# First loads, warm-up products, the second chunk's normalization and the last products of a fused attention and squared-ReLU layer, reordered

## The chip, the core and the metric

The kernel runs on one core of one Trainium2 chip. The metric is the device time of one execution in microseconds (us); lower is better. A profiled execution gives a trace, whose times start at the first instruction. The engines are named as in the profile: PE (TensorE matmul), PEld (its weight load), DVE (VectorE), ACT (ScalarE), POOL (GpSimd), SP (SyncE, which issues most DMAs).

## What is computed

```python
xn = layernorm(x)                                   # x: 2048 x 512
q, k, v = split(xn @ wqkv)                          # 32 heads of 16
s = softmax(q k^T / 4) v, heads joined, @ wo
g = silu(relu(xn @ w1 + b1)**2 @ w2 + b2)           # 512 -> 1792 -> 512
out = x + s * g
```

All of it is float32. The kernel reaches that accuracy by splitting each operand of a linear product into a high part (a cast to the format fp32r) and a low part (the operand less the high part) and adding three products: high by high, high by low, low by high.

## The kernel before

The 2048 rows are worked in four chunks (c = 0 to 3) of 512 rows, each of four tiles of 128 rows. The kernel has three stages. The first, up to about 140 us, normalizes the chunks and makes values, keys and queries. The second, most of the time, runs scores, exponentials and products with the values in 128 turns, with the other branch's matmuls between them. The third, the last 20 us, projects what is left and writes the output. The order of instructions on each engine is the order of the program text (a manual schedule); an engine that waits holds everything behind it in its own queue.

**First loads** (`load_x` L127, `load_w` L140, L427 to L431). SP issues the first chunk's tile 0 and tile 1 as two DMAs of 256 KB (L135), then the upper half of the value weights (L136, `load_w("v", sp, (0,))`), tiles 2 and 3 (one DMA of 512 KB, L132), the lower half of the value weights, the key weights, chunk 1 and b1; the query weights follow at L446.

**Warm-up** (L437 to L439). Eleven products of the identity with itself, into a bank that nobody reads. The profile shows each as two instructions.

**Normalization** (`norm` L162). A generator of three steps: statistics on DVE (L169), their aggregation on DVE and a square root on ACT (L172, L176), and the reciprocal, a correction of three small DVE instructions and the normalized tile on DVE (L178 to L186). `next(parts)` runs one step where it stands.

**Chunk 0** (L440 to L464). `split_w("v", (k,))` (L155) casts slice k of the weights on ACT (L98, tile `wf1h`) and makes the low part on POOL (L104, `wf1l`). `transpose_tile(i)` (L212) transposes tile i of the first pair on PE (L217), copies the high part on ACT (L219, tile `KA`) and makes the low part on DVE (L220). Then two accumulations of twelve products each are interleaved (L458 to L460, the products at L111), twenty of them ahead of the transposes of tiles 2 and 3 (`transpose(0, 1)`, L197 to L210, PE line L204). The order of ACT's queue is: slice 0, tile 0, slice 1, tile 1, square root for tiles 2 and 3, slices 2 and 3.

**The loop over the chunks** (L472 to L512). For each chunk: values tile by tile (`end_value`, L238), then for each g of 0 to 3 the keys and the queries (`keyquery`, L245: twelve products on PE, a cast on ACT, L98, a subtraction on DVE, L104, a DMA on SP). Between them stand steps of the next chunk's normalization (`parts`). For chunk 0, three of the six steps for chunk 1 run behind the values of tiles 2 and 3, and three behind the keys and queries of g = 0 and the keys of g = 1. At g = 2 the next chunk is transposed (L492 to L494).

**The end** (L812 to L864). `end_rest(i, src)` (L740) scales a finished projection of tile i of chunk 2 on DVE (L743) and has POOL issue a DMA that adds it to the output (L744). `h` and `l` are high and low part of the last head's normalized result (L843 to L846); `nvalid` (L847) is the flag that decides whether the general path runs; it does not run here. The last four tiles, those of chunk 3, each take three products (L657 in `group`), a DVE multiplication by the gate (L859), and an addition of x. The products are made in pairs of tiles: both high products of two tiles, then the low product of each. Tile 0's addition is POOL's, those of tiles 2 and 3 are DVE's (L863), and tile 1 is added by a DMA that POOL issues (L861) to what `add_gated` (L645, L651) wrote there in the second stage. ACT issues the other three output DMAs (L864).

Of the kernel before, what the change touches and what calls it, by code (L numbers as in the profile page):

```python
# [28 lines left out]
OP = mybir.AluOpType  # L29
# [8 lines left out]
NC = S // 512  # L38
# [35 lines left out]
def fast_path(tc, sb, ps, env):  # L74
    nc = tc.nc
    ident, vt, nvalid, stat = (env[n] for n in ("ident", "vt", "nvalid", "stat"))
    kdram, qdram, xdram, udram, zdram, gdram = (
        env[n] for n in ("kdram", "qdram", "xdram", "udram", "zdram", "gdram"))
    x, wqkv, wo, w1, b1, w2, b2, out = (
        env[n] for n in ("x", "wqkv", "wo", "w1", "b1", "w2", "b2", "out"))  # L80
    mm = nc.tensor.matmul
    dve, act, pool, sp = nc.vector, nc.scalar, nc.gpsimd, nc.sync
# [3 lines left out]
    def t(shape, dt, tag):  # L86

        cnt[0] += 1
        p = ps if tag in ("S", "lin", "acc") else sb
        if tag in BUFS:  # L90
            turn[tag] = turn.get(tag, -1) + 1
            n = turn[tag] % BUFS[tag]
            tag = f"{tag}{places[n] if tag == 'S' else n}"
        return p.tile(shape, dt, tag=tag, name=f"{tag}_{cnt[0]}")
# [19 lines left out]
    def run(gen):  # L114
        for _ in gen:
            pass
# [10 lines left out]
    def load_x(c):  # L127
        for i in range(2):
            a = xload[c, i] = t([128, 2, 512], FT, f"P{4 + 2 * (c % 2) + i}")
            r = c * 512 + i * 256  # L130
            if c or i:
                sp.dma_start(a, x[r:r + 256].rearrange("(a p) d -> p a d", p=128))  # L132
            else:
                for j in range(2):
                    sp.dma_start(a[:, j], x[128 * j:128 * j + 128])  # L135
                load_w("v", sp, (0,))  # L136

    w_tags = {"v": "wf1", "k": "wf2", "q": "h"}
# [1 line left out]
    def load_w(which, eng, parts=range(2)):  # L140
        o = {"q": 0, "k": 512, "v": 1024}[which]
        if which in wraw:
            pass
        elif which == "v":
            a = t([128, 4, 512], FT, "KA2")
            wraw[which] = [a[:, :2], a[:, 2:]]
        elif which == "k":
            wraw[which] = [t([128, 2, 512], FT, "QA") for _ in range(2)]
        else:
            wraw[which] = [t([128, 2, 512], FT, "wr") for _ in range(2)]  # L150
        for i in parts:
            eng.dma_start(wraw[which][i], wqkv[i * 256:i * 256 + 256, o:o + 512]
                          .rearrange("(a p) f -> p a f", p=128))

    def split_w(which, ks=range(4)):  # L155
        if which not in wsp:
            tiles = [[t([128, 2, 512], FR, f"{w_tags[which]}{p}{i}") for i in range(2)] for p in "hl"]
            wsp[which] = [[a[k // 2][:, k % 2] for k in range(4)] for a in tiles]
        for k in ks:
            split(wsp[which][0][k], wsp[which][1][k], wraw[which][k // 2][:, k % 2], act, pool)  # L160
# [51 lines left out]
    def transpose_tile(i):  # L212

        h, low = xT[0]
        pt = t([128, 4, 128], FT, "S")
        for k in range(4):
            nc.tensor.transpose(pt[:, k], xnorm[0, 0][:, i, 128 * k:128 * k + 128], ident)  # L217
        s = slice(128 * i, 128 * i + 128)
        act.copy(h[:, :, s], pt)  # L219
        dve.tensor_tensor(low[:, :, s], pt, h[:, :, s].bitcast(FT), op=OP.subtract)  # L220
# [214 lines left out]
        pool.memset(part[:, :, H * 17:], 0.0)  # L435
    pool.memset(stat, 1.0)
    idle = t([128, 512], FT, "lin")  # L437
    for _ in range(11):
        mm(idle[:, :128], ident, ident, start=True, stop=True)  # L439
    parts = [norm(0, (0,)), norm(0, (1,)), norm(0, (2, 3))]  # L440
    for n in (0, 0, 1, 1, 0, 1):
        next(parts[n])

    pool.tensor_copy(t([128, 1], FT, "okm"), xnorm[0, 0][:, 1, :1])
    split_w("v", (0,))
    load_w("q", sp)  # L446
    xT_tiles(0)
    transpose_tile(0)
    split_w("v", (1,))
    next(parts[2])  # L450
    transpose_tile(1)
    next(parts[2])
    split_w("v", (2, 3))
    run(parts[2])
    late = [(k, 0, 1) for k in range(4)]
    todo = [[(k, a, 0) for n in (0, 2) for a in range(2) for k in (n, n + 1)],
            [(k, a, 0) for a in range(2) for k in range(4)]]
# [14 lines left out]
    parts = chain(norm(1, (0, 1)), norm(1, (2, 3)))  # L472
    for c in range(NC):
        for i in range(4):
            if c or i > 1:
                end_value(c, i, start_value(c, i))
                next(parts, None)
            if c == 0:
                if i == 3:
                    next(parts, None)  # L480
                if i == 2:
                    split_w("q")
            if c == 1 and i == 0:
                bp = t([128, 14], FT, "acc")
                nc.tensor.transpose(bp, b1raw, ident[:14, :14])
                dve.tensor_copy(b1t, bp)
        if c == 3:
            act.activation(t([128, 1], FT, "warm"), eps, AF.Exp)
            for _ in range(2):
                load_piece()  # L490
        for g in range(4):
            if g == 2 and c + 1 < NC:  # L492
                for i in range(2):
                    transpose(c + 1, i)  # L494
                if c < 2:
                    save_xT(c + 1)
                if c + 2 < NC:
                    parts = chain(norm(c + 2, (0, 1)), norm(c + 2, (2, 3)))
            for which in "kq":
                if c == 3 and g == 3 and which == "q":  # L500
                    exps(0, 0, scores(0, 0))
                    exps(0, 1, scores(0, 1))
                keyquery(c, g, which, "acc" if (c, g, which) == (3, 3, "q") else "S")
                next(parts, None)
            if g == 0 and c + 2 < NC:
                load_x(c + 2)
            if g == 3 and c == 2:
                turn["KA"] = 1
                load_ka(0, 0)
                load_qa(0, 0)  # L510
            if g == 1 and c == 3:
                split_piece(act)  # L512
# [75 lines left out]
    wos, gsb, pend, onorm, base = [None], {}, {}, {}, {}  # L588
# [56 lines left out]
    def add_gated(c, i):  # L645
        o = t([128, 2, 512], FT, "T")
        dve.scalar_tensor_tensor(o, spare, 0.5, gsb[c, i], op0=OP.mult, op1=OP.mult)
        dve.tensor_tensor(base[c, i], base[c, i], o, op=OP.add)
        if c < 3 or i == 0:
            r = 512 * c + 256 * i  # L650
            (sp if (c, i) == (1, 1) else pool).dma_start(out[r:r + 256].rearrange("(a p) d -> p a d", p=128), base[c, i])  # L651

    cut = [slice(128 * i, 128 * i + 128) for i in range(4)]

    def group(dst, lhs, rhs, start=True, stop=True, todo=((0, 0), (0, 1), (1, 0))):
        for n, (a, b) in enumerate(todo):
            mm(dst, lhs(a), rhs(b), start=start and n == 0, stop=stop and n == len(todo) - 1)  # L657
# [7 lines left out]
    wlast = []  # L665
# [62 lines left out]
    n = turn["S"]  # L728
    places[:] = [(n - 2) % 3, (n - 1) % 3, n % 3]
    BUFS["S"], turn["S"] = 2, 1  # L730
    spare = ps.tile([128, 2, 512], FT, tag=f"S{places[2]}", name="spare")
# [8 lines left out]
    def end_rest(i, src):  # L740

        o = t([128, 512], FT, f"wf2{'hl'[i // 2]}{i % 2}")
        dve.scalar_tensor_tensor(o, src, 0.5, gsb[2, i // 2][:, i % 2], op0=OP.mult, op1=OP.mult)  # L743
        pool.dma_start(out[1024 + 128 * i:1152 + 128 * i], o, accum_op=OP.add)  # L744

    turn_ends_first = [False]
    for n in range(TURNS):
        i = 4 * n
# [44 lines left out]
        if n == TURNS - 1:  # L793
            two = t([128, 2, 512], FT, "S")
# [18 lines left out]
    zc, r = t([128, 16], FT, "zc"), t([128, 16], FT, "rc")  # L813
    ok, okm, ones = t([128, 80], FT, "ok"), t([128, 1], FT, "okm"), t([128, 1], FT, "ones")
    dve.memset(ones, 1.0)
    h, l = t([128, 512], FR, "wf1h0"), t([128, 512], FR, "wf1l0")
# [4 lines left out]
    lins = [small[:, 1], t([128, 512], FT, "lin"), t([128, 512], FT, "acc"), two[:, 0]]  # L821
# [7 lines left out]
    for i in range(4):  # L829
        for j in range(4):  # L830
            mm(small[32 * j:32 * j + 32, 0, cut[i]], r[:, 4 * i + j:4 * i + j + 1].broadcast_to([128, 32]), ident,
               start=True, stop=True)
# [2 lines left out]
    dve.tensor_scalar(ok[:, 0:32], stat[:, 0:32], Z_MIN, None, op0=OP.is_ge)  # L835
    dve.tensor_scalar(ok[:, 32:80], stat[:, 32:80], BIG, None, op0=OP.is_le)
    dve.tensor_reduce(okm, ok, axis=AX.X, op=OP.min)
    end_rest(3, spare[:, 1])
    pn = lins[1][0:1, 16:17]
    mm(pn, okm, ones, start=True, stop=True)  # L840
    rest(1, two[:, 1])
# [3 lines left out]
    for s in half:  # L845
        dve.tensor_tensor(l[:, s], ou[:, s], h[:, s].bitcast(FT), op=OP.subtract)  # L846
    dve.tensor_copy(nvalid, pn)  # L847
    end_rest(1, two[:, 1])


    o = [t([128, 512], FT, f"P{2 + i}") for i in range(4)]
    for j in range(2):
        for todo in ((0, 0), (0, 1)), ((1, 0),):
            for i in (2 * j, 2 * j + 1):
                group(lins[i], lambda p: (h, l)[p][:, cut[i]], lambda p: wlast[0][:, p],
                      start=len(todo) == 2, stop=len(todo) == 1, todo=todo)
        for i in (2 * j, 2 * j + 1):
            rows = out[1536 + 128 * i:1664 + 128 * i]
            dve.scalar_tensor_tensor(o[i], lins[i], 0.5, gsb[3, j][:, i % 2], op0=OP.mult, op1=OP.mult)  # L859
            if i == 1:  # L860
                pool.dma_start(rows, o[i], accum_op=OP.add)  # L861
            else:
                (dve if i else pool).tensor_tensor(o[i], o[i], base[3, j][:, i % 2], op=OP.add)  # L863
                act.dma_start(rows, o[i])  # L864


def general_path(tc, dram, nvalid, ident, vt, kdram, qdram, gdram, x, wo, out):
# [109 lines left out]
```

## Time and profile before

| | |
|---|---|
| median of 3 executions | 1273.52 us (1272.1 to 1274.15) |
| the profiled execution's own time | 1273.92 us |
| its span in the trace | 1272.2 us |
| PE busy | 1257.9 us |
| ACT busy | 1033.8 us |
| DVE busy | 682.0 us |
| POOL busy | 259.0 us |
| DMA traffic | 137.30 MB |

The span runs from the first to the last instruction; the execution's own time is 1.7 us longer. Rows of instruction groups give the line, engine, operation, output and inputs, then the total and the mean time. A timeline row starts with the start and the duration in us; instructions that follow each other in one queue are merged into one row, with their number behind an x. The chain of waits follows the work that ended last back from the end. A table by windows gives, for each stretch, its length, the busy time of each engine with the number of instructions, the clock that PE was granted (1.00 is full), the mean busy share of the DMA engines (rounding lets it pass 1) and GB/s.

### The profile page before, as it was taken

The page shows a single profiled execution, that of the slowest core. Times are in us where ns is not written, and L with a number is a line of the kernel's source. Part 1 is how long each engine was busy: PE and PEld are TensorE (multiplying, and loading weights), DVE is VectorE, ACT ScalarE, POOL GpSimd, SP SyncE. Part 2 cuts the span into 40 slices and gives each one's busy share as a digit, 9 for nine tenths or more (in the row PEclk, how much of TensorE's full clock was granted, in tenths as well). Part 3 has the DMA queues.
Part 4 walks back from the last instruction along what each step waited for, and adds up shares of the span by engine and source line. Part 5 has one row for each costly group of instructions (what it writes and reads, how often), then busy time and mean ns, then how long its engine had stood idle before and what let it go on. Part 6 is the DMA issues. An engine that isn't in the chain of part 4 may idle for free.

```text
span 1272.2 us, 24755 instructions
## 1 busy us (share of the span) xinstructions
PE 1257.9 (99%) x9909; PEld 721.7 (57%) x9909; DVE 682.0 (54%) x1064; ACT 1033.8 (81%) x1122; POOL 259.0 (20%) x150
## 2 busy tenths in 40 slices
PE   8999999999999999999999999999999999999997
PEld 6888754555555555555555555555555555545553
DVE  6542255555555655545455555555654545566655
ACT  4222488988999898989998899899898989998883
POOL 5000022222121231303023211220320312322112
PEclk8999999999999999999999999999999999999998
DMA  6664513231333222221423122332222222463445
GB/s 240 232 232 179 213 60 105 59 93 43 93 125 109 59 83 67 57 82 53 155 76 109 44 92 59 93 125 90 61 73 76 59 89 60 142 216 118 150 129 118
DMA packets 84955, 137.30 MB, mean 108 GB/s; under 512 B 26074, under 2 KB 40424, under 8 KB 83300
## 3 DMA queue, kind: packets, MB, share of 16 engines
q1 hardware_dynamic: 81684, 126.25, 30.8%
q0 software_dynamic: 2720, 8.65, 2.4%
q8 instruction: 78, 1.28, 0.4%
q10 hardware_dynamic: 432, 0.79, 0.2%
q14 instruction: 41, 0.34, 0.1%
HBM read 94.24 MB, written 41.41 MB: 107 GB/s over the span
## 4 chain that ended last, share of the span: by engine, by line
PE 96%; DVE 1%; ACT 1%; POOL 0%; DMA 0%; issue 0%; SPq 0%; DVEq 0%; ACTq 0%
PE acc L531 36%; PE spare L326 26%; PE S L278 16%; PE S L111 9%; PE lin L278 7%; DVE P L301 1%; PE S L204 0%; DMA KA<-in_A_wqkv_dram 0%; PE acc L111 0%; POOL hl L104 0%; ACT P L282 0%; PE lin L111 0%; ACT wf2h L98 0%; PE spare L657 0%; PE S L657 0%
## 5 line engine op out<-in xcount | busy, mean ns | idle before, releaser
L282 ACT ACTIVATE P<-S 128x1024 f32<-128x1024 f32 x768 | 732.4, 1020 | 66.8 <-PE S L278 65.9
L301 DVE COPY P<-lin 128x512 f32<-128x512 f32 x512 | 354.1, 692 | 464.3 <-PE lin L278 333.5
L531 PE MATMUL acc<-P,vt 128*32 128x512 f32 x4096 | 466.0, 595 | 0.0
L278 PE MATMUL S<-QA,KA 64*128 64x512 f32 x1536 | 332.1, 421 | 0.2 <-ACT P L282 0.2
L282 ACT ACTIVATE P<-P 128x1024 f32<-128x1024 f32 x256 | 271.4, 1060 | 44.1 <-DVE P L301 44.0
L531 PEld LDWEIGHTS acc<-P,vt 128*32 128x32 f32 x4096 | 120.2, 110 | 273.0 <-issue 273.0
L278 PEld LDWEIGHTS S<-QA,KA 64*128 64x128 f32 x1536 | 145.3, 184 | 157.8 <-ACT P L282 140.3
L278 PE MATMUL lin<-QA,KA 64*128 64x512 f32 x512 | 213.4, 417 | 1.1 <-DVE P L301 0.5
L104 POOL TENSOR_TENSOR wf1l<-wr,wf1h 128x1024 fp32r<-128x1024 f32 x28 | 66.8, 2385 | 404.3 <-DVE wf1h L100 135.3
L326 PE MATMUL spare<-xl,wf1h 64*128 64x512 f32 x504 | 122.6, 400 | 0.0
L104 POOL TENSOR_TENSOR hl<-T,hh 128x1024 fp32r<-128x1024 f32 x28 | 67.6, 2414 | 242.3 <-DVE hh L100 145.6
L104 POOL TENSOR_TENSOR wf2l<-wr,wf2h 128x1024 fp32r<-128x1024 f32 x28 | 66.7, 2382 | 207.2 <-PE acc L531 138.7
L326 PE MATMUL spare<-wf2l,hh 64*128 64x512 f32 x448 | 107.2, 399 | 0.0
L278 PEld LDWEIGHTS lin<-QA,KA 64*128 64x128 f32 x512 | 94.2, 184 | 22.9 <-DVE P L301 14.3
L326 PE MATMUL spare<-xh,wf1l 64*128 64x512 f32 x504 | 96.2, 392 | 0.0
L326 PE MATMUL spare<-xh,wf1h 64*128 64x512 f32 x504 | 95.6, 390 | 0.0
L326 PE MATMUL spare<-wf2h,hh 64*128 64x512 f32 x448 | 87.7, 392 | 0.0
L326 PE MATMUL spare<-wf2h,hl 64*128 64x512 f32 x448 | 84.5, 390 | 0.0
L326 PEld LDWEIGHTS spare<-xl,wf1h 64*128 64x128 f32 x504 | 66.8, 184 | 8.9
L326 PEld LDWEIGHTS spare<-xh,wf1h 64*128 64x128 f32 x504 | 59.8, 185 | 9.4
L326 PEld LDWEIGHTS spare<-xh,wf1l 64*128 64x128 f32 x504 | 59.8, 185 | 8.7
L326 PEld LDWEIGHTS spare<-wf2l,hh 64*128 64x128 f32 x448 | 59.8, 185 | 7.8
(201 smaller groups left out, 958.3 us busy)
## 6 DMA issues: line engine op xcount, KB each, us to landing
wr<-in_B_w_dram SPq DMA_DIRECT2D x56, 512.0 KB
KA<-kd SPq DMA_DIRECT2D x64, 256.0 KB
QA<-qd SPq DMA_DIRECT2D x128, 128.0 KB
kd<-P SPq DMA_DIRECT2D x15, 512.0 KB
qd<-P SPq DMA_DIRECT2D x15, 512.0 KB
u<-ud SPq DMA_DIRECT2D x15, 512.0 KB
xd<-KA SPq DMA_DIRECT2D x4, 1024.0 KB
gd<-y SPq DMA_DIRECT2D x8, 512.0 KB
```

Of the source, the lines that this page charges most:

```text
L104: leng.tensor_tensor(lo, src, hi.bitcast(FT), op=OP.subtract)
L111: mm(dst, lhs(a, k), rhs(b, k), start=n == 0, stop=n == len(todo) - 1)
L278: mm(dst, k[r, p, 128 * (kb % 8):128 * (kb % 8) + 128], q[r, p], start=True, stop=True)
L282: act.activation(ptile[i, p], src, AF.Exp, scale=SCALE)
L301: dve.tensor_copy(ptile[i, p][:, hp], single)
L326: mm(bank, self.lhs(a, k)[r], self.rhs(b, k)[r], start=n == 0 and self.at[other] == 0, stop=n == len(self.todo[half]) - 1 and self.at[othe ...
L531: mm(acc[0][32 * j:32 * j + 32], vt[:, kb, o:o + 32], ptile[i, j // 2][:, j % 2], start=kb == 0, stop=kb == NK - 1)
```

## The change

Four places change.

1. `load_x` issues tiles 0 and 1 of chunk 0 as one DMA of 512 KB; the upper half of the value weights follows it as before.
2. The warm-up has 16 products. ACT casts slices 0 and 1 of the value weights ahead of tile 0's copy; three more warm-up products stand between the transposes of tile 0 and tile 1; slice 2 is cast ahead of tile 1's copy, slice 3 behind it, and the square root for tiles 2 and 3 comes behind slice 3.
3. In chunk 0's round, no step of chunk 1's normalization runs behind the values any more; all six run behind the keys and queries of g = 0, 1 and 2, one behind each. The transposes of chunk 1 move from g = 2 to g = 3 in that round; the other rounds keep theirs.
4. At the end, `end_rest(3)` moves from ahead of `h` and `l` to the place of `end_rest(1)`, and `end_rest(1)` to behind tile 0's multiplication. The products are made tile by tile. POOL adds x to tiles 0 and 1, DVE to tiles 2 and 3 behind all four multiplications, and ACT issues all four output DMAs in order. `add_gated` (L645) no longer writes tiles 0 and 1 of chunk 3 to the output during the second stage (L651, one DMA of 512 KB by POOL at 1168.1 us): it was there so that tile 1's last DMA had something to add to.

```diff
--- before.py
+++ after.py
@@ -128,11 +128,8 @@
         for i in range(2):
             a = xload[c, i] = t([128, 2, 512], FT, f"P{4 + 2 * (c % 2) + i}")
             r = c * 512 + i * 256
-            if c or i:
-                sp.dma_start(a, x[r:r + 256].rearrange("(a p) d -> p a d", p=128))
-            else:
-                for j in range(2):
-                    sp.dma_start(a[:, j], x[128 * j:128 * j + 128])
+            sp.dma_start(a, x[r:r + 256].rearrange("(a p) d -> p a d", p=128))
+            if c == i == 0:
                 load_w("v", sp, (0,))
 
     w_tags = {"v": "wf1", "k": "wf2", "q": "h"}
@@ -435,22 +432,27 @@
         pool.memset(part[:, :, H * 17:], 0.0)
     pool.memset(stat, 1.0)
     idle = t([128, 512], FT, "lin")
-    for _ in range(11):
-        mm(idle[:, :128], ident, ident, start=True, stop=True)
+
+    def keep_clock(n):
+        for _ in range(n):
+            mm(idle[:, :128], ident, ident, start=True, stop=True)
+
+    keep_clock(16)
     parts = [norm(0, (0,)), norm(0, (1,)), norm(0, (2, 3))]
     for n in (0, 0, 1, 1, 0, 1):
         next(parts[n])
 
     pool.tensor_copy(t([128, 1], FT, "okm"), xnorm[0, 0][:, 1, :1])
-    split_w("v", (0,))
+    split_w("v", (0, 1))
     load_w("q", sp)
     xT_tiles(0)
     transpose_tile(0)
-    split_w("v", (1,))
+    keep_clock(3)
+    split_w("v", (2,))
     next(parts[2])
     transpose_tile(1)
+    split_w("v", (3,))
     next(parts[2])
-    split_w("v", (2, 3))
     run(parts[2])
     late = [(k, 0, 1) for k in range(4)]
     todo = [[(k, a, 0) for n in (0, 2) for a in range(2) for k in (n, n + 1)],
@@ -474,12 +476,10 @@
         for i in range(4):
             if c or i > 1:
                 end_value(c, i, start_value(c, i))
-                next(parts, None)
-            if c == 0:
-                if i == 3:
+                if c:
                     next(parts, None)
-                if i == 2:
-                    split_w("q")
+            if c == 0 and i == 2:
+                split_w("q")
             if c == 1 and i == 0:
                 bp = t([128, 14], FT, "acc")
                 nc.tensor.transpose(bp, b1raw, ident[:14, :14])
@@ -489,7 +489,7 @@
             for _ in range(2):
                 load_piece()
         for g in range(4):
-            if g == 2 and c + 1 < NC:
+            if g == (2 if c else 3) and c + 1 < NC:
                 for i in range(2):
                     transpose(c + 1, i)
                 if c < 2:
@@ -646,7 +646,7 @@
         o = t([128, 2, 512], FT, "T")
         dve.scalar_tensor_tensor(o, spare, 0.5, gsb[c, i], op0=OP.mult, op1=OP.mult)
         dve.tensor_tensor(base[c, i], base[c, i], o, op=OP.add)
-        if c < 3 or i == 0:
+        if c < 3:
             r = 512 * c + 256 * i
             (sp if (c, i) == (1, 1) else pool).dma_start(out[r:r + 256].rearrange("(a p) d -> p a d", p=128), base[c, i])
 
@@ -835,7 +835,6 @@
     dve.tensor_scalar(ok[:, 0:32], stat[:, 0:32], Z_MIN, None, op0=OP.is_ge)
     dve.tensor_scalar(ok[:, 32:80], stat[:, 32:80], BIG, None, op0=OP.is_le)
     dve.tensor_reduce(okm, ok, axis=AX.X, op=OP.min)
-    end_rest(3, spare[:, 1])
     pn = lins[1][0:1, 16:17]
     mm(pn, okm, ones, start=True, stop=True)
     rest(1, two[:, 1])
@@ -845,23 +844,19 @@
     for s in half:
         dve.tensor_tensor(l[:, s], ou[:, s], h[:, s].bitcast(FT), op=OP.subtract)
     dve.tensor_copy(nvalid, pn)
-    end_rest(1, two[:, 1])
-
-
+    end_rest(3, spare[:, 1])
     o = [t([128, 512], FT, f"P{2 + i}") for i in range(4)]
-    for j in range(2):
-        for todo in ((0, 0), (0, 1)), ((1, 0),):
-            for i in (2 * j, 2 * j + 1):
-                group(lins[i], lambda p: (h, l)[p][:, cut[i]], lambda p: wlast[0][:, p],
-                      start=len(todo) == 2, stop=len(todo) == 1, todo=todo)
-        for i in (2 * j, 2 * j + 1):
-            rows = out[1536 + 128 * i:1664 + 128 * i]
-            dve.scalar_tensor_tensor(o[i], lins[i], 0.5, gsb[3, j][:, i % 2], op0=OP.mult, op1=OP.mult)
-            if i == 1:
-                pool.dma_start(rows, o[i], accum_op=OP.add)
-            else:
-                (dve if i else pool).tensor_tensor(o[i], o[i], base[3, j][:, i % 2], op=OP.add)
-                act.dma_start(rows, o[i])
+    for i in range(4):
+        group(lins[i], lambda p: (h, l)[p][:, cut[i]], lambda p: wlast[0][:, p])
+        dve.scalar_tensor_tensor(o[i], lins[i], 0.5, gsb[3, i // 2][:, i % 2], op0=OP.mult, op1=OP.mult)
+        if i < 2:
+            pool.tensor_tensor(o[i], o[i], base[3, 0][:, i], op=OP.add)
+        if i == 0:
+            end_rest(1, two[:, 1])
+    for i in range(4):
+        if i > 1:
+            dve.tensor_tensor(o[i], o[i], base[3, 1][:, i % 2], op=OP.add)
+        act.dma_start(out[1536 + 128 * i:1664 + 128 * i], o[i])
 
 
 def general_path(tc, dram, nvalid, ident, vt, kdram, qdram, gdram, x, wo, out):
```

## The prediction

> **What bounds the kernel now.** I read the page first, then the chain of waits in order of time for the first 32 us and the last 30, then tables by windows with the granted clock, then the timelines of single engines.
>
> ```profile
> span 1272.2 us, 24755 instructions
> PE   8999999999999999999999999999999999999997
> PE 96%; DVE 1%; ACT 1%; POOL 0%; DMA 0%; issue 0%; SPq 0%; DVEq 0%; ACTq 0%
> 38.58 13.61 PE S L111 x60
> ```
>
> PE is full in all slices but the first and the last, and 96% of the chain is its own. The chain row shows the projections running without a gap. So whatever the first 40 us gain or lose reaches the end in full, a hole torn into a full stretch costs its whole length, and the second stage is touched by nothing here. Three places decide: the start, chunk 0's round, the last 10 us.
>
> Windows of 3.41 us, laid where the granted clock changes (length, busy time and count of PE, PEld, DVE, ACT and POOL, clock, DMA share, GB/s):
>
> ```profile
> 5.95:9.36 3.41, 2.09 (x12) 1.14 (x10) 2.01 (x7) 1.63 (x4) 1.11 (x2) 1.00 1.02 378
> 9.36:12.77 3.41, 2.84 (x7) 1.78 (x6) 2.88 (x10) 1.65 (x4) 1.89 (x3) 0.50 1.05 396
> 12.77:16.18 3.41, 3.41 (x9) 2.53 (x9) 2.92 (x3) 0.15 (x1) 2.22 (x2) 0.50 1.05 385
> 16.18:19.59 3.41, 3.33 (x19) 2.50 (x17) 0.00 (x0) 0.97 (x2) 0.00 (x0) 1.00 0.25 94
> 36.66:40.07 3.41, 3.41 (x25) 3.11 (x24) 2.67 (x6) 2.52 (x3) 0.00 (x0) 1.00 0.88 277
> 1262.05:1265.46 3.41, 1.15 (x5) 0.57 (x4) 3.23 (x6) 0.00 (x0) 2.30 (x3) 1.00 0.87 166
> ```
>
> The first of them for the transposes alone (L217; PE, PEld, clock, DMA):
>
> ```profile
> 5.95:9.36 3.41, 1.31 (x8) 0.84 (x8) 1.00 1.02 378
> ```
>
> A window in which PE was busy for 2.09 us is followed by two at half clock, and a full one (12.77 to 16.18) by full clock again. In the cold full window a product of 512 columns takes 3.41 us / 8 = 0.43 us; at full clock the chain's 13.61 us for 60 make it 0.23 us.
>
> The warm-up products themselves, ahead of 5.5 us and around 6 us:
>
> ```profile
> L439 PE MATMUL lin<-ident 128*128 128x128 f32 x19 | 4.4, 430 | 1.4 <-POOL ident masks.py:199 1.4
> L439 PE MATMUL lin<-ident 128*128 128x128 f32 x3 | 0.7, 346 | 0.0
> ```
>
> They shorten at the end, so I take the clock as really half until 5.95 us, where the table says 1.00 for want of an earlier record. One takes 4.4 / 19 = 0.23 us there, with overlap 0.21, and about half of that at full clock, 0.11.
>
> **The start.** The chain of waits; then what SP waited for and its next DMA, and POOL's and DVE's timelines:
>
> ```profile
> 1.69 6.02 DMA KA<-in_A_wqkv_dram
> 7.73 0.62 ACT wf1h L98
> 8.35 0.49 ACT KA L219
> 8.87 0.69 DVE KA L220
> ...
> 17.70 0.89 PE S L204 x8
> ...
> 25.79 5.01 POOL hl L104 x4
> ```
> ```profile
> SPq L152 <- DMA P<-in_A_x_dram: 1.0, 1, 1.0
> 9.12 0.37 SPq L152 DMA_DIRECT2D wr<-in_A_wqkv_dram  x1
> 12.48 2.51 POOL L104 TENSOR_TENSOR wf1l<-KA,wf1h 128x512 fp32r<-128x512 f32 x2 [1.52 <-ACT wf1h L98]
> 12.51 1.25 DVE L181 SCALAR_TENSOR_TENSOR rs<-rs 128x2 f32<-128x2 f32 x1
> 35.58 0.15 DVE L178 RECIPROCAL rs<-rs 128x2 f32<-128x2 f32 x1
> ...
> 36.16 0.16 DVE L181 SCALAR_TENSOR_TENSOR rs<-rs 128x2 f32<-128x2 f32 x1
> 36.35 1.00 DVE L186 TENSOR_SCALAR T<-P,mv,rs 128x512 f32<-128x512 f32 x2
> 37.49 0.69 DVE L104 TENSOR_TENSOR P<-S,P 128x512 fp32r<-128x512 f32 x1
> ```
>
> The value weights land at 7.71 us, tile 0's copy lets the first product start at 8.85, and twenty products and their waits last until 17.6, most of them at half clock.
>
> *First loads.* One SP issue of some 0.45 us goes; the weights can land at best that much earlier. The windows show the DMA engines full (share 1.02) from 5.95 us, so most of it should be lost; I take 7.7 us as before, and -0.45 as the other end. Tile 0 now waits for both tiles; its transposes wait for the longer warm-up anyway.
>
> *Warm-up.* 32 instructions from 1.37 us: 21 at 0.21 until 5.95, 11 at 0.11, end at 7.2. Transposes of tile 0 to 7.7, three more products (6 x 0.11 = 0.65), transposes of tile 1 to about 8.8. PE is occupied without a gap to there, where the weights hold it anyway: the new products cost nothing.
>
> *Casts.* ACT: slices 0 and 1 from 7.73 (0.5 us each as they follow each other, as the 0.49 in the chain), tile 0's copy to 9.3. First product 9.3, 0.45 later than before. The third waits for DVE's low part (0.69): 10.05; the fourth ends 10.5. The fifth needs tile 1's copy, which now stands in ACT's queue behind slice 2, so behind the lower half of the weights. SP's DMA at 9.12 had waited for a load of x, so tiles 2 and 3 landed then; 512 KB more at about 0.4 MB/us is 1.3 us: 10.4. Cast and copy: 11.55. PE idles 1.05 us there. Then 16 products x 0.23 = 3.7: the transposes of tiles 2 and 3 start at **15.2 instead of 17.5: -2.3 us**, if the clock stays up. DVE must have those tiles normalized by then: it starts the aggregation at 12.3 (behind tile 1's low part), and POOL's last subtraction ends at about 13.7 (casts at 11.05 and 12.07, 1.26 each). In the rows above, DVE's L181 took 1.25 us beside POOL's subtraction and 0.16 where POOL was idle, so I let the corrections end with POOL, near 13.7, and two tiles (1.00) at 14.7. If POOL holds DVE for one subtraction more, 16.0, and the gain is 1.5.
>
> The clock: in the window from 9.36 PE would idle 1.3 of 3.41 us, 61% busy; before, 2.09 of 3.41 (also 61%) lowered the clock, yet 1.31 us of those were transposes, and the window 36.66 to 40.07, which has 16 transposes (1.91 us, the row of 36.67 below) and 1.5 us of products, did not lower it. If transposes count little, the window that fell was at 23%, and the limit lies between 34% (1.15 of 3.41 at the end, followed by half clock) and 44%; then 61% holds. If they count, it may fall, ten products cost 0.43 until 16.18, and the gain is 0.8. Bounds of the start: -3.2 (all sixteen cold products warm) to 0.
>
> **Chunk 0's round.** The six steps for chunk 1 now run one behind each key or query, so the last, which makes tiles 2 and 3 of chunk 1, stands in DVE's queue behind the subtraction of the queries of g = 2, and the transposes of these tiles follow on PE at once. The DVE rows from 35.58 above are its queue just ahead of the transposes before; ACT's and PE's beside it:
>
> ```profile
> 36.87 0.59 ACT L98 CAST P<-S 128x512 fp32r<-128x512 f32 x1 [1.94 <-PE S L111]
> 36.67 1.91 PE L204 MATMUL S<-ident,T 128*128 128x128 f32 x16
> ```
>
> Before, the tiles end at 37.35 and PE reaches their transposes at about 37.55: hidden by 0.2 us. Now, with T the time at which PE starts the transposes: ACT's cast T + 0.2, DVE's subtraction T + 0.82, reciprocal 0.6 later, the tiles 0.77 behind that: T + 2.2 to 3.2. PE does the first eight transposes by T + 0.95, waits until T + 2.8 for tile 2 and 3.25 for tile 3. **+1.9 us**, by the same rows' own spacing. No other work of PE stands behind these transposes that could go first. What is cheaper in return, DVE free beside POOL's subtractions from 21 to 31 us, gives PE nothing: the chain there is POOL's own subtractions (5.01 us for four), which start behind ACT's casts of the key weights as before and move with them.
>
> And the clock: from T to T + 3.7 PE does nothing but 16 transposes and the wait. If transposes count little, nearly every position of a 3.41 us window leaves one under 44%; the clock halves for a window, and 3.41 us at half speed is **+1.7 us**. Bounds: 0 (no drop) and 3.4 (two windows, as at 9.36).
>
> The Trainium skill (TensorE: Matmul & The Clock Gate, section "Why this matters for your kernels") asks only that PE have no gap over some 3 us between bursts; the wait is 1.9, so by that rule nothing would be added, and the sum would be 1.7 lower. The same page (Part 4: PE-mode transpose) says that transposes do not count as busy in the same way, and then the gap is 3.7 us and the clock falls. The trace speaks against the first rule: in the window from 5.95 no gap can be over 1.32 us, and the clock fell.
>
> **The end.** DVE's, POOL's and ACT's rows (ACT's with shortest, median and longest in ns, first and last start):
>
> ```profile
> 1257.71 0.68 DVE L743 SCALAR_TENSOR_TENSOR wf2l<-spare,y 128x512 f32<-128x512 f32 x1
> 1261.43 0.83 POOL L744 DMA_DIRECT2D out_dram<-wf2h  x1 [1.90 <-DVE wf2h L743]
> 1262.44 1.27 POOL L863 TENSOR_TENSOR P<-P,KA 128x512 f32<-128x512 f32 x1 [0.17 <-DVE P L859]
> 1263.68 0.85 POOL L861 DMA_DIRECT2D out_dram<-P  x1
> L864 ACTq DMA_DIRECT2D out_dram<-P x3: 338/338/381, 1263.7 to 1265.8; - x3
> 1261.60 0.69 DVE L859 SCALAR_TENSOR_TENSOR P<-S,gl 128x512 f32<-128x512 f32 x1 [0.46 <-PE S L657]
> 1265.05 0.69 DVE L863 TENSOR_TENSOR P<-P,KA 128x512 f32<-128x512 f32 x1
> ```
>
> Tile 0's products are ready 1 us earlier, but DVE is not free: `end_rest(3)` (0.68) stood in a wait for PE and now stands ahead of tile 0. From 1260.5 to 1265.74 DVE had seven operations (0.65 us as they follow each other) and some 0.6 us of waits, of which the row shows 0.46; now it has eight and no wait: it ends at about 1265.7 as before. POOL has DMA, addition, DMA, addition: the first three at the times of the rows above, the second addition 1264.6 to 1265.9. ACT issues in order, so tile 1 goes at 1265.95, tiles 2 and 3 behind it at 0.38 (0.34 and the step to the next): the last at 1266.7 instead of 1265.75. Against that, one of POOL's adding DMAs fewer is in flight when the last data move. **+0.6 us**; bounds +1.0 (the later issue in full) and -0.7 (the DMA that goes, if the queue sets the end). The output DMA of the second stage that goes was hidden behind PE: nothing.
>
> The Trainium skill (GPSIMD Engine Reference, "Specifications") says that POOL's SBUF interfaces are shared with DVE's operations of two SBUF inputs. By it tile 3's addition would wait for POOL's second one; it would still be ready for ACT's turn at 1266.7, so the sum stays.
>
> **Sum.** 1273.92 - 2.3 + 1.9 + 1.7 + 0.6 = 1275.8 against the profiled execution's own time, which is 0.4 over the median: **1275.4 us**, 0.15% over 1273.52. A measurement of this kernel can tell about 0.2% (2.5 us) from no change.
>
> **The rivals.** (1) *No drop of the clock in chunk 0's round*: 1.7 less, 1273.7. For it the short wait; against it 3.7 us without a product. (2) *The start gains little*: the clock falls there too, since 61% may be too little, so -0.8 instead of -2.3: 1276.9, clearly slower; it decides if transposes count as busy, which puts the limit above 61%. (3) *The transposes of chunk 1 do not wait*, because I misplace the last step by one: 1.9 and 1.7 less, 1271.8, faster than before. Against it stands the order of the loop: six steps, six places, the sixth directly ahead of the transposes.
>
> **Chances.** The forecast 0.47, (1) 0.22, (2) 0.23, (3) 0.08. With about 1 us of spread in each, faster by over 0.2% (under 1271.0) has 0.08, within 0.2% 0.58, slower 0.34. The range reaches from (3) to (2) with the later end of the DMAs and a smaller gain: 1271.8 to 1277.9; the forecast alone spans 1274.2 to 1276.6.
>
> **What would show it.** At the start: first product near 9.3 at full clock, a hole of 1 us near 10.5 ended by ACT's copy of tile 1, the transposes of tiles 2 and 3 near 15.2. Near 39.8 us a wait of PE at L204 for DVE L186, about 1.85 us, and half clock for a window behind it. At the end ACT's last issue near 0.95 us later in relation to the final products. I am wrong if PE passes L204 without a wait, if the clock stays at 1.00 there, or if the weights land well ahead of 7.7 us.

## The result and the profile after

The changed kernel takes 1274.66 us (median of 22 executions, 1273.8 to 1275.59), the kernel before 1272.39 us (22, 1271.22 to 1274.25): a ratio of 1.0016, 95% interval 1.001 to 1.0023, so 2.3 us slower. The profiled execution after took 1274.63 us with a span of 1272.9 us; the one before had 1273.92 and 1272.2. That one of before lies 1.5 us over its median, which matters below.

The page after: span, and the chain by engine.

```profile
span 1272.9 us, 24787 instructions
...
PE 96%; DVE 2%; POOL 1%; issue 1%; ACT 0%; DVEq 0%; ACTq 0%; POOLq 0%
```

PE is still 96% of the chain.

**The start.** Timelines of the changed kernel:

```profile
1.38 6.79 PE L438 MATMUL lin<-ident 128*128 128x128 f32 x32 [1.38 <-POOL ident masks.py:199]
4.46 0.69 DVE L166 BATCH_NORM_STATS2 st<-P 128x6 f32<-128x512 f32 x1 [3.58 <-DMA P<-in_A_x_dram]
5.81 1.96 SPq L149 DMA_DIRECT2D wr<-in_A_wqkv_dram  x2
6.40 1.12 ACT L98 CAST wf1h<-KA 128x512 fp32r<-128x512 f32 x2
8.00 0.60 PE L214 MATMUL S<-ident,T 128*128 128x128 f32 x4
...
9.46 1.27 PE L111 MATMUL lin<-wf1h,KA 128*128 128x512 f32 x4
10.57 0.63 PE L111 MATMUL acc<-wf1h,KA 128*128 128x512 f32 x2
...
14.71 1.12 PE L201 MATMUL S<-ident,T 128*128 128x128 f32 x8 [0.31 <-DVE T L183]
```

SP's issue at 5.81 had waited for the value weights: they land at 5.8 us, not at 7.7, and ACT casts both slices with no wait for them. The price of the single DMA is tile 0 at 4.46 instead of 3.45. The first product starts at 9.46, the fifth at 10.57 without the hole that I had put there, and the transposes of tiles 2 and 3 at 14.71; before it was 17.54. PE waits for DVE in the end, not for weights.

Where the landing comes from shows in the DMA engines ahead of it. Two stretches of the kernel before, then the same two of the changed one (the last two figures are the DMA share and GB/s):

```profile
3.50:4.00 0.50, 0.50 (x4) 0.50 (x4) 0.50 (x1) 0.00 (x0) 0.00 (x0) 1.00 0.64 152
4.00:4.50 0.50, 0.50 (x4) 0.50 (x4) 0.47 (x3) 0.10 (x1) 0.00 (x0) 1.00 0.45 143
```
```profile
3.50:4.00 0.50, 0.50 (x4) 0.50 (x4) 0.00 (x0) 0.00 (x0) 0.00 (x0) 1.00 1.03 397
4.00:4.50 0.50, 0.50 (x4) 0.50 (x4) 0.04 (x1) 0.00 (x0) 0.00 (x0) 1.00 1.06 410
```

From 3.5 to 6 us the DMA engines moved 192 GB/s on average before and 401 after. The 0.5 MB between them takes 1.3 us at 0.4 MB/us, an estimate from these rows; with the issue 0.4 us earlier (1.27 instead of 1.69 us) it accounts for most of the 1.9 us.

**Chunk 0's round.** DVE and PE around the transposes of chunk 1, then three windows of 3.41 us there:

```profile
39.34 1.03 PE L201 MATMUL S<-ident,T 128*128 128x128 f32 x8
...
40.20 0.69 DVE L104 TENSOR_TENSOR P<-S,P 128x512 fp32r<-128x512 f32 x1 [1.87 <-ACT P L98]
...
41.58 1.00 DVE L183 TENSOR_SCALAR T<-P,mv,rs 128x512 f32<-128x512 f32 x2
42.19 1.11 PE L201 MATMUL S<-ident,T 128*128 128x128 f32 x8 [1.82 <-DVE T L183]
```
```profile
38.32:41.73 3.41, 2.05 (x14) 1.56 (x12) 1.40 (x7) 1.89 (x3) 0.00 (x0) 1.00 0.43 160
41.73:45.15 3.42, 2.96 (x17) 2.61 (x18) 2.82 (x6) 1.02 (x1) 0.00 (x0) 1.00 0.38 153
45.15:48.56 3.41, 3.41 (x16) 2.82 (x16) 2.35 (x4) 0.59 (x1) 0.00 (x0) 1.00 1.02 420
```

The wait of 1.82 us is there, for the row that was named. The clock is 1.00 in all three windows: it did not fall.

**The end.** The changed kernel's rows, and of the kernel before the row that starts the same stretch (the multiplication by the reciprocals):

```profile
1258.06 0.76 DVE L842 TENSOR_TENSOR P<-S,P 128x256 f32<-128x256 f32 x2 [0.97 <-PE lin L839]
...
1261.29 1.60 POOL L853 TENSOR_TENSOR P<-P,KA 128x512 f32<-128x512 f32 x1
...
1262.92 3.62 ACTq L859 DMA_DIRECT2D out_dram<-P  x4
1263.13 1.88 POOL L853 TENSOR_TENSOR P<-P,KA 128x512 f32<-128x512 f32 x1
1263.35 2.82 DVE L858 TENSOR_TENSOR P<-P,KA 128x512 f32<-128x512 f32 x2
```
```profile
1258.77 0.76 DVE L843 TENSOR_TENSOR P<-S,P 128x256 f32<-128x256 f32 x2 [0.38 <-PE lin L840]
```

From that row to the end of the span it was 1272.2 - 1258.77 = 13.4 us, and is 1272.9 - 1258.06 = 14.8. POOL's second addition takes 1.88 us (1.27 before, alone), and DVE's two take 2.82 together instead of 1.4: it looks as if they hold each other up, which e8 puts to the test. ACT's last issue starts near 1266.2, right behind DVE's last addition (1263.35 + 2.82 = 1266.17) and 8.1 us behind the row instead of 7.0.

### The profile page after: what moved, and what is told of

It reads as the page before. It is cut to its first block, busy times and chain, and to the rows that moved or that the text cites. A ratio compares the mean times of both kernels' runs of the same rounds, so it can differ in the third digit from the quotient of the medians.

```text
span 1272.9 us, 24787 instructions
## 1 busy us (share of the span) xinstructions
PE 1257.1 (99%) x9925; PEld 722.8 (57%) x9925; DVE 678.4 (53%) x1064; ACT 1034.6 (81%) x1122; POOL 259.0 (20%) x149
## 3 DMA queue, kind: packets, MB, share of 16 engines
q10 hardware_dynamic: 576, 1.05, 0.2%
## 4 chain that ended last, share of the span: by engine, by line
PE 96%; DVE 2%; POOL 1%; issue 1%; ACT 0%; DVEq 0%; ACTq 0%; POOLq 0%
PE acc L531 36%; PE spare L323 27%; PE S L275 16%; PE S L111 9%; PE lin L275 7%; DVE P L298 1%; PE lin L438 1%; PE S L201 0%; POOL hl L104 0%; PE acc L111 0%; DVE P L851 0%; POOL wf2l L104 0%; PE spare L657 0%; DVE rs L177 0%; DVE KA L217 0%
## 5 line engine op out<-in xcount | busy, mean ns | idle before, releaser
L98 ACT CAST P<-S 128x512 fp32r<-128x512 f32 x30 | 17.7, 588 | 57.2 <-PE S L111 57.2
```

Source lines behind the costliest of these rows:

```text
L98: act.copy(dst, src)
```

## The experiments

My theory after the result: three parts that add. The start gains 2.8 us against the profiled execution of before but about 1 in the median; the round costs 1.8 to 2; the end costs up to 1.4. The first four runs undo one part each, or do one alone. Times are medians, 11 or 12 executions of each kernel except where said. "Of before" is the ratio to the executions of the kernel before that ran beside that experiment: medians 1272.65 us (33, e1 to e4), 1272.91 (35, e5 to e8) and 1273.61 (15, e9 and e10). The intervals reach about 1 us to either side, and the changed kernel ran at another time, so differences of a few tenths of a us tell nothing.

**e1: the normalization undone.**

```diff
-                if c:
-                    next(parts, None)
-            if c == 0 and i == 2:
-                split_w("q")
+                next(parts, None)
+            if c == 0:
+                if i == 3:
+                    next(parts, None)
+                if i == 2:
+                    split_w("q")
...
-            if g == (2 if c else 3) and c + 1 < NC:
+            if g == 2 and c + 1 < NC:
```

> The changed kernel with its third part undone: chunk 1's normalization and transposes stand where they stood before, all else as changed. Theory (three parts that add: start a gain, chunk 0's round a loss of 1.8 us, end a loss of 1.4 us): PE's wait at the transposes of chunk 1 for DVE's normalized tile (1.82 us in the changed kernel) is gone, and the time is 1.8 us under the changed kernel's, some 0.4 us over the kernel before (ratio about 1.0003). Rival (the wait only pulls forward a wait that would come later, such as the projections waiting for evictions): the time stays within 0.5 us of the changed kernel's, ratio about 1.0016.

Measured: 1272.26 us, 0.9999 of before (0.999 to 1.0008), 2.4 us under the changed kernel. PE from 33 to 40 us (busy times, clock, DMA), where the transposes now are:

```profile
33.00:40.00 7.00, 7.00 (x40) 6.02 (x39) 5.38 (x13) 3.11 (x4) 0.00 (x0) 1.00 1.01 320
```

No wait at all, and nothing later takes its place: 2.4 us came back for a wait of 1.82, the same within the noise.

**e2: the end undone** (`add_gated`, L834 to the end of the function as before).

> The changed kernel with its fourth part undone: the last 10 us as before. Theory: from the first multiplication by the reciprocals on DVE to the end of the span 13.4 us as before, instead of 14.8, and the time 1.4 us under the changed kernel's (ratio to before about 1.0007). Rival (the end is set by the queue of output DMAs and not by their issue, and the profiled execution caught a late one): under 0.5 us of difference, ratio about 1.0014.

Measured: 1273.93 us, 1.001 of before (1.0001 to 1.0019), 0.7 us under the changed kernel. The stretch is 13.4 us again (1272.1 - 1258.73). So the direction holds, and the size lies between theory and rival. The profiles tell why: the unchanged new end took 14.8 us in two kernels (changed, e1), 14.4 in e9, 14.1 in e3 and 13.9 in e7; the old one 13.4 to 13.7 in six. (Each is the span less the start of that DVE row.) One profile is not enough for a tail of DMAs; the mean difference, 14.4 - 13.5, is 0.9.

**e3: the start undone** (`load_x`, and L438 to L456 as before).

> The changed kernel with its first and second part undone: loads, warm-up and casts as before. Theory: 2.8 us slower than the changed kernel where the clock falls as it did in the profiled execution of before, less where the clock's window lies better; as the medians of the whole change differ by 2.3 us and the other two parts cost 3.2, the start is worth about 1 us in the median, so a ratio of about 1.0025 to before. Rival (the start's 2.8 us are there in each execution, and something not seen costs 1.9): ratio about 1.004.

Measured: 1275.79 us, 1.0025 of before (1.0016 to 1.0034), 1.1 us over the changed kernel. In this execution the old start kept its clock. PE's rows, and three windows from the wait in chunk 0's round:

```profile
9.03 1.49 PE L111 MATMUL lin<-wf1h,KA 128*128 128x512 f32 x4 [0.76 <-ACT KA L219]
10.35 0.63 PE L111 MATMUL acc<-wf1h,KA 128*128 128x512 f32 x2
12.59 1.48 PE L111 MATMUL lin<-wf1h,KA 128*128 128x512 f32 x4 [1.60 <-ACT wf1h L98]
...
16.20 1.03 PE L204 MATMUL S<-ident,T 128*128 128x128 f32 x8
```
```profile
38.39:41.81 3.42, 3.38 (x20) 2.66 (x18) 1.06 (x4) 1.34 (x4) 0.00 (x0) 1.00 0.73 289
41.81:45.22 3.41, 1.64 (x11) 1.49 (x12) 3.23 (x9) 1.49 (x2) 0.00 (x0) 1.00 0.48 192
45.22:48.63 3.41, 3.41 (x16) 2.81 (x15) 1.78 (x3) 1.12 (x2) 0.00 (x0) 1.00 0.64 264
```

The transposes of tiles 2 and 3 start at 16.20, 1.3 us ahead of the execution profiled first: that is about what the clock cost there. Against this the new start's 14.7 to 15.0 (changed kernel, e1, e2, e4) is a gain of 1.2 to 1.5. The wait of 1.60 us is ACT's: slices 2 and 3 stand behind the square root for tiles 2 and 3.

**e4: the start alone** (the kernel before with both start edits).

> The kernel before with the first and second part of the change alone. Theory: the transposes of chunk 0's tiles 2 and 3 start near 14.7 us, the end is as before, and the median is about 1 us under before (ratio 0.9992), with a smaller spread, since the clock no longer falls in some executions. Rival (a gain of 2.8 us in each execution): ratio 0.9978.

Measured: 1271.63 us, 0.9993 of before (0.9984 to 1.0002), spread 1271.28 to 1272.48: 1.2 us where before had 3.

The mean granted clock of every execution supports the theory. One window at half clock takes 3.41 x 0.5 / 1272 = 0.0013 off that mean. The half clock behind the last product, 4.0 to 7.8 us long in the profiles, leaves 0.9969 or more where the clock fell nowhere else, so a mean of 0.996 or less points to a fall (0.997 may hide one). Of the 83 executions of before that ran beside the experiments, 38 are at 0.996 or less, with a median of 1273.8 us, and the other 45 have 1272.0. None of e4's eleven is that low. So a good part of the start's 1 us seems to be the falls that it avoids and not the earlier loads; no run separates the two.

The next four look for the mechanism inside each part.

**e5: the load alone.**

```diff
-            if c or i:
-                sp.dma_start(a, x[r:r + 256].rearrange("(a p) d -> p a d", p=128))
-            else:
-                for j in range(2):
-                    sp.dma_start(a[:, j], x[128 * j:128 * j + 128])
+            sp.dma_start(a, x[r:r + 256].rearrange("(a p) d -> p a d", p=128))
+            if c == i == 0:
                 load_w("v", sp, (0,))
```

> The kernel before with the first part of the change alone: tiles 0 and 1 in one DMA. Theory (the single DMA is what lets the value weights land near 5.8 us instead of 7.7): the weights land near 5.8 us, tile 0's statistics start near 4.5 instead of 3.45, and the transposes of tiles 2 and 3 start at 15.2 to 16 us where the clock stays up. Rival (the weights land earlier because of other things, such as the order of the casts or the query weights' issue): landing at 7.7 as before, and the later tile 0 makes the start about 0.5 us slower.

Measured: 1272.39 us, 0.9997 (0.9988 to 1.0006). SP's issue that waits for the value weights, PE, and the windows:

```profile
5.87 1.72 SPq L149 DMA_DIRECT2D wr<-in_A_wqkv_dram  x2
```
```profile
10.17 0.63 PE L111 MATMUL acc<-wf1h,KA 128*128 128x512 f32 x2
12.40 1.98 PE L111 MATMUL lin<-wf1h,KA 128*128 128x512 f32 x4 [1.60 <-ACT wf1h L98]
```
```profile
6.35:9.76 3.41, 1.76 (x12) 1.38 (x12) 3.03 (x11) 2.16 (x5) 1.01 (x2) 1.00 1.05 386
9.76:13.17 3.41, 1.79 (x7) 0.87 (x6) 2.88 (x9) 1.58 (x4) 2.41 (x3) 1.00 1.04 385
13.17:16.59 3.42, 3.42 (x9) 2.66 (x9) 2.47 (x3) 0.00 (x0) 1.77 (x2) 0.50 0.87 321
```

The single DMA by itself brings the weights from 7.7 to 5.9 us: for the landing the theory is confirmed and the rival out. It gains little alone, since the old order of the casts keeps its 1.60 us wait, and the clock fell at 13.17 in this execution (transposes at 17.6), the slowest of the eleven (1274.5). The theory's 15.2 to 16 us with the clock up was not seen.

**e6: warm-up and casts alone** (L437 to L454 of the changed kernel in the kernel before).

> The kernel before with the second part of the change alone: 16 + 3 warm-up products and the order of the casts, with two DMAs for tiles 0 and 1. Theory (as predicted for these loads): weights at 7.7 us, first product near 9.3, PE idle for 1 us near 10.5 because tile 1's copy stands behind slice 2 and so behind the lower half of the weights (10.5), transposes of tiles 2 and 3 near 15.2; the clock does not fall, so the spread is small, and the median is 0.4 to 0.8 us under before. Rival (the longer warm-up does not keep the clock): half clock in some executions, transposes at 16 to 17.5 there, and the spread of before (3 us).

Measured: 1271.9 us, 0.9994 (0.9986 to 1.0003). ACT and PE:

```profile
8.02 1.14 ACT L98 CAST wf1h<-KA 128x512 fp32r<-128x512 f32 x2 [2.36 <-DMA KA<-in_A_wqkv_dram]
9.06 0.58 ACT L219 CAST KA<-S 128x512 fp32r<-128x512 f32 x1
10.70 0.62 ACT L98 CAST wf1h<-KA 128x512 fp32r<-128x512 f32 x1 [1.06 <-DMA KA<-in_A_wqkv_dram]
11.22 0.58 ACT L219 CAST KA<-S 128x512 fp32r<-128x512 f32 x1
```
```profile
11.86 0.73 PE L111 MATMUL acc<-wf1h,KA 128*128 128x512 f32 x2 [0.70 <-ACT KA L219]
```

This is the start that I predicted, with the old loads: weights at 8.0, tile 1's copy behind slice 2 and so behind the lower half of the weights, PE waiting 0.70 us for it; transposes at 15.62. One of 12 executions took 1274.63, at a mean clock of 0.995, so the longer warm-up does not always keep the clock; the others took 1271.21 to 1272.82.

**e7: the normalization one step earlier.**

```diff
-                if c:
+                if c or i == 3:
                     next(parts, None)
```

> The changed kernel with one step of chunk 1's normalization more ahead: the first of the six runs behind the value of tile 3, so the last runs behind the keys of g = 2 instead of behind its queries. The transposes stay at g = 3. Theory (PE waits because the last step stands behind the subtraction of the queries of g = 2 on DVE): the wait of 1.82 us goes entirely, and the time falls by 2.0 to 2.3 us to that of the kernel whose normalization was undone (1272.3). Rival (the wait comes from moving the transposes to g = 3, for instance through the PSUM banks or the order of the evictions): the wait stays.

Measured: 1272.45 us, 0.9999 (0.9991 to 1.0008), 2.2 us under the changed kernel. PE:

```profile
39.59 1.91 PE L201 MATMUL S<-ident,T 128*128 128x128 f32 x16
```

All sixteen transposes run in one piece at g = 3. One place in the queue decides, not the move of the transposes.

**e8: one addition for POOL** (tile 1's goes to DVE).

```diff
-        if i < 2:
+        if i == 0:
             pool.tensor_tensor(o[i], o[i], base[3, 0][:, i], op=OP.add)
...
-        if i > 1:
-            dve.tensor_tensor(o[i], o[i], base[3, 1][:, i % 2], op=OP.add)
+        if i:
+            dve.tensor_tensor(o[i], o[i], base[3, i // 2][:, i % 2], op=OP.add)
```

> The changed kernel with tile 1's addition on DVE instead of POOL; POOL adds tile 0 alone. Theory (POOL's second addition and DVE's first hold each other up: 1.88 and 2.22 us instead of 1.27 and 0.69): DVE's three additions take 0.7 us each without a hole, ACT's last issue comes 0.7 us earlier against the first multiplication by the reciprocals (7.4 us behind it instead of 8.1), and the end is 0.4 to 0.8 us shorter. Rival (the time of the landing is set by the adding DMAs in the queue): ACT's last issue is earlier, but the end of the span stays 14.1 to 14.8 us behind that point.

Measured: 1274.74 us, 1.0014 (1.0005 to 1.0022), the changed kernel's time. DVE and ACT (issues with shortest, median and longest in ns, first and last start):

```profile
1263.79 1.87 DVE L858 TENSOR_TENSOR P<-P,KA 128x512 f32<-128x512 f32 x3
```
```profile
L859 ACTq DMA_DIRECT2D out_dram<-P x4: 338/385/1859, 1263.4 to 1267.0; - x4
```

DVE's additions are free of the hole: three in 1.87 us where two took 2.82. So POOL and DVE did hold each other up, but no time came of it: one of ACT's issues, tile 2's, now took 1859 ns, and the last starts 8.5 us behind the multiplication by the reciprocals. The end of the span is 14.6 us behind it (1273.1 - 1258.51), as the rival had it, but not by the rival's path: ACT's last issue came later, not earlier. In all twelve profiles the span ends 5.8 to 6.8 us behind ACT's last issue, so the end goes with that issue. What held the long one, and which of the queued DMAs, is not shown.

Two runs for what was left: the clock, and whether the new products do anything.

**e9: a longer wait** (4 executions).

```diff
+                if (c, g, which) == (0, 2, "q"):
+                    scr = t([128, 512], FT, "ou1")
+                    for _ in range(4):
+                        dve.tensor_tensor(scr, xnorm[1, 0][:, 0], xnorm[1, 0][:, 1], op=OP.add)
                 next(parts, None)
```

> The changed kernel with four more additions of 128x512 on DVE ahead of the last step of chunk 1's normalization (their result is read by nobody), so that PE's wait at the transposes grows by 4 x 0.6 to 0.7 = 2.4 to 2.8 us, from 1.8 to some 4.4. Theory (a longer stretch without products lowers the clock, the forecast's mechanism with too short a wait): half clock for a window of 3.4 us behind the wait, and 4.2 us over the changed kernel in all (2.5 for the wait, 1.7 for the clock). Rival (the clock does not react to this wait at all): the clock stays at 1.00, and the time is 2.5 us over the changed kernel.

Measured: 1278.91 us, 4.25 us over the changed kernel (3.4 by the two ratios to before), 1.0043 of before (1.0028 to 1.0059). The profiled execution is the slowest of the four, 1279.58 us. What PE waited for (total, times, longest), and windows:

```profile
PE S L201 <- DVE T L183: 4.6, 1, 4.6
```
```profile
40.01:43.42 3.41, 0.33 (x4) 0.10 (x1) 3.15 (x5) 1.14 (x2) 0.00 (x0) 1.00 0.60 236
43.42:46.83 3.41, 1.89 (x9) 1.89 (x10) 2.98 (x9) 0.00 (x0) 0.00 (x0) 0.50 0.00 0
46.83:50.25 3.42, 3.42 (x10) 2.65 (x9) 1.29 (x2) 1.01 (x1) 0.00 (x0) 0.50 0.46 192
50.25:53.66 3.41, 3.41 (x17) 2.81 (x16) 1.69 (x3) 0.59 (x1) 0.00 (x0) 1.00 1.02 411
```

With the wait at 4.6 us one window is almost empty, and half clock follows for two. A wait can lower the clock here: one of 4.6 us did, one of 1.8 us did not in four profiles (changed, e2, e3, e8). The time agrees with the theory's 4.2 us by the medians and lies between theory and rival by the ratios; the clock decides against the rival.

**e10: no new products** (both start edits in the kernel before, with `keep_clock(11)` and no `keep_clock(3)`).

> The kernel before with the one DMA for tiles 0 and 1 and the new order of the casts, but with the eleven warm-up products of before and none between the transposes. Theory (the products only keep the clock; the order of the casts and the load make the rest): transposes of tiles 2 and 3 at 14.4 to 15 us where the clock stays up, and half clock for one or two windows in a part of the executions, so a spread of 2 to 3 us and a median of 0.3 to 1 us under before. Rival (the new products cost PE time at the start): 0.5 us faster than with them, 1.5 us under before, with a small spread.

Measured: 1271.57 us, 0.9985 of before (0.9976 to 0.9994), spread 1270.55 to 1272.04: faster than the kernel before beside it, and the same time as e4 with the new products. The ratio is lower than e4's because the kernel before took 1273.61 here and 1272.65 there. In the profiled execution the clock fell all the same. PE's busy time over 4 us and the clock, then the transposes of tiles 2 and 3:

```profile
8.00:12.00 4.00, 3.42 (x15) 2.56 (x14) 3.45 (x9) 2.46 (x5) 3.05 (x4) 0.70 1.04 393
```
```profile
15.61 1.04 PE L201 MATMUL S<-ident,T 128*128 128x128 f32 x8
```

They start at 15.61 here, 0.6 to 0.9 us behind the kernels with the new products, which the medians do not show. Neither theory nor rival got the size right: the spread is small and the gain over e4 nil.

## Why the prediction was right in the sum, and where its terms were wrong

The forecast was 1275.4 us, 0.15% slower; measured were 1274.66 and 0.16%. Two of its terms were wrong and cancelled, and that the sum came out is luck: the clock's +1.7 did not come, and the start gained 1.0 in place of 2.3. Of the three signs that were to show the prediction wrong, two came: the clock stayed at 1.00 in chunk 0's round, and the weights landed 1.9 us ahead of 7.7.

- **The wait in chunk 0's round: right.** Forecast 1.9 us from the spacing of six rows; PE's record shows 1.82, and taking it away was worth 2.4 (e1) and 2.2 us (e7). Rival (3), that the step is misplaced, is out.
- **The fall of the clock there (+1.7): wrong.** The step "nearly every position of a 3.41 us window leaves one under 44%" failed, and with it the limit that it rests on, with transposes counting little. No profile with this wait (changed, e2, e3, e8) shows half clock there; all 44 executions of the changed kernel, e2 and e8 have a mean clock of 0.997 or 0.998, 28 of them 0.998, which leaves no room for a fall. In e3 PE was busy 1.64 of 3.41 us, 1.11 of it with transposes. In e8 a window held almost nothing but transposes (all of PE's work, then L201 alone), and the clock stayed:

```profile
40.00:43.41 3.41, 1.59 (x14) 1.28 (x12) 3.03 (x9) 1.25 (x3) 0.00 (x0) 1.00 0.62 246
40.00:43.41 3.41, 1.52 (x12) 1.01 (x10) 1.00 0.62 246
```

These are 0.07 us of products, 2%, and no fall; in e5 the window from 9.76 had 1.79 us of products, 52%, and no transpose, and the clock fell behind it. A share of products alone is not the limit. Rival (1), given 0.22, was the true case here. The rule of the Trainium skill that was weighed (TensorE: Matmul & The Clock Gate, "Why this matters for your kernels": no gaps over some 3 us) agrees with these runs, 1.8 and 4.6 us; it does not cover the start, where the clock fell in e5 with no wait over 1.6.

- **The start (-2.3): right against the profiled execution (-2.8), too large for the median.** I summed against one execution in which the clock had fallen for two windows and took 0.4 us off for its place among three. Its true distance to the median of before is 1.5. The start alone is worth 1.0 us (e4), its undoing costs 1.1 (e3); rival (2) had the size, not the reason: the new start kept its clock in all seven profiles of it, while the old one often kept its own as well (e4).
- **The loads: wrong.** I put the landing of the weights at 7.7 us, with 7.25 as the other end. It was 5.8, outside those bounds; e5 shows that the single DMA does it. The step that failed is that the DMA engines are full, "so most of it should be lost": they were full from 5.95 us, but not from 3.5 to 6 us, where the time came from. The early landing removed the hole by ACT's order, forecast at 1.05 us and 0.70 in e6. The longer warm-up and DVE's normalization took up most of the gain.
- **The end (+0.6): right in size, by another path.** It is 0.7 in the median (e2), inside the noise, and 0.9 in the profiles. ACT's last issue comes 1.1 us later against the row, forecast 0.95. But POOL's second addition was done at 1265.0 (1263.13 + 1.88), and by ACT's turn, two issues of 0.38, tile 3 would have gone near 1265.8. It went at 1266.2, right behind DVE's last addition: the step "it would still be ready for ACT's turn" failed. POOL and DVE slow each other (1.88 us instead of 1.27, 2.82 for two instead of 1.4), which agrees with the sentence of the Trainium skill weighed there (GPSIMD Engine Reference, "Specifications"), and without that the tail is as long (e8).

The sum of the measured parts is -1.0 + 2.4 + 0.7 = 2.1 us against 2.27 of the medians, so within the noise they add.

## What to carry to other kernels

When work is moved later, write down for each consumer which instruction stands directly ahead of its producer in the producer's queue: a step that is off the critical path by a whole stage is back on it when its last part stands behind the eviction that ends the stage. Before summing against one profiled execution, look at how far it lies from the median, and whether something that changes from execution to execution (here the clock at the start) is in it. Before calling a load bound by the DMA engines, read their share over the whole stretch from its issue to its landing, not only at the end of it. The version to keep here is the load in one DMA with the new order of the casts, without the moved normalization and the new end: e10's 1271.57 us. That is 0.9985 of the kernel before beside it, and 0.9992 of the median of before beside e4.

## What the runs showed of the hardware that was not expected

One DMA of 512 KB in place of two of 256 KB ahead of it in SP's queue let the next load land at 5.8 to 5.9 us instead of 7.7 to 8.0 (changed kernel and e5 against before and e6), though its issue came only 0.4 us earlier. Behind the two the DMA engines were partly idle from 3.5 to 6 us (shares of 0.45 to 0.98 over half a us each), behind the one they were full (1.03 to 1.06). Why they ran dry is open.

The busy share of a window does not tell alone whether the clock falls behind it: 2.09 of 3.41 us (before) and 1.79 (e5) were followed by half clock, 1.76 (e5's window ahead), 2.05 (changed), 1.64 (e3) and 1.59 (e8) were not. Nor does the share of products without the transposes: 0.07 us (e8) kept the clock and 1.79 (e5) did not. What the windows differ in is open.
